# Products with the values by tile shape: one wide and one narrow task per tile instead of two halves of heads

## The chip, the cores and the metric

The kernel runs on one core of one Trainium2 chip. The core has five engines with queues of their own: TensorE (PE, with its weight loads shown as PEld), VectorE (DVE), ScalarE (ACT), GpSimd (POOL) and SyncE (SP), which here only issues transfers. Time is device time of one execution in microseconds (us); the lower the better. Three executions of the kernel before gave 310.41, 311.28 and 312.01 us, so the median is 311.28 us.

## The reference

Block-sparse attention feeds a soft mixture of experts. There are 4 batches, 8 heads, 768 positions in 24 blocks of 32, and a head dimension of 64. A query block sees its own block and both neighbours, the first and the last block, and three sampled blocks; the first and the last query block see everything.

```
scores = scale * q @ k.T                       # scale = 1/8
mask   = |blk_i - blk_j| <= 1, or blk_i or blk_j is 0 or 23, or blk_j in sampled[blk_i]
attn   = softmax(where(mask, scores, -1e9))
x      = (attn @ v)  as [4*768, 8*64]
logits = x @ phi                               # 32 slots: 8 experts x 4
slot_input = softmax(logits, over rows).T @ x
slot_out   = relu(slot_input @ w1[e]) @ w2[e]  # per expert, hidden width 1024
out    = softmax(logits, over slots) @ slot_out
```

Everything is in float32.

## The kernel before

**Tiles and units.** The 22 middle query blocks of a batch go in pairs, called units: 64 queries of all 8 heads. For a unit the kernel gathers the keys of each query block into a staging buffer (`kst`, eight blocks wide: fixed neighbours by POOL, sampled ones by ACT or POOL), multiplies (`s`, line 521), takes maxima, exponentials (`p`) and transposes them on DVE (`ptt`). The three sampled value blocks of a query block are copied into `vrs` by POOL (line 466). The other value blocks are read where they lie, in `v`. Two units make a tile of 128 queries (`T`); the first tile of a batch has one unit and shares its rows with the first and last query blocks, whose dense attention is a task of its own (`avd`). So a batch has five tiles of two units, and four batches have 20.

**Products with the values.** `av_heads(T, rs_)` (line 623) multiplies the turned weights by the values for the heads in `rs_`: `r` is 0 or 1, a half of the heads. The result lies in one PSUM tile `av` of two banks, one for each `g`, which is also the half of PE's rows (partitions 0 to 63 or 64 to 127) that the product uses; each half `r` has its own 130 columns of a bank. The 65th column of each head's values is one, so that the sums of the softmax come out beside the products. Three shapes of matmul follow each other within a call:

- the first and the last value block, for all 128 queries of the tile: shape 64*128 (64 rows, 128 columns of PE's array), lines 628 to 632;
- the two value blocks that both query blocks of a unit see, for 64 queries: shape 64*64, lines 633 to 639;
- the outer neighbour and the three sampled blocks, for 32 queries each: shape 64*32, lines 640 to 656.

A call in the program shows in the profile as two matmuls and two weight loads. The first product into a region has `start`, the last `stop`. Before, `plan_av` (line 658) makes two PE tasks for a tile of two units, one for each half `r`. Each goes through all three shapes. The last tile of the last batch is split in another way (`T.split`) and keeps two halves.

**Order of the work.** The order on each engine is laid out in advance by `Plan.run` (line 94). Every task has a possible engine with an assumed duration, the tasks it depends on, buffers that it takes from pools, and a due number (`key`, with a correction in `BEHIND`). The planner takes the task that can start first by its own reckoning, and among those that could start within 0.03 us the one with the lowest due number. Each engine then runs its tasks in that order and waits for semaphores where the real times differ. The two halves have an assumed PE time of 2.36 us each and the due number n + 0.5; both depend on the turned weights (`T.turned`), on the copies into `vrs` (`T.staged`) and on the batch's values. PE tasks that may come between are the scores of a later unit (due n + 1 and so on), the transposes of finished rows (`mxt`), logits and slot sums. `av` has one buffer, released by the DVE task that divides by the sums (`av_out`, lines 608 to 610). Loads of weights for the mixture are spread over attention and tied to PE tasks of the plan; when attention has ended, its buffers are reused for the remaining weights.

After attention come the experts' two layers and the combination, with weights loaded on the SP queue all the way.

Of the kernel before, what the change touches and what calls it, by code (L numbers as in the profile page):

```python
# [11 lines left out]
F32 = mybir.dt.float32  # L12
I32 = mybir.dt.int32
F32R = mybir.dt.float32r
# [6 lines left out]
BLK, NB, NR = 32, 24, 3  # L21
P = 128
# [6 lines left out]
D1 = D + 1  # L29

VPOS = lambda k: (k - 1) % (NB + 1)
# [48 lines left out]
class Plan:  # L80
# [6 lines left out]
    def add(self, f, opts, deps, key, acq=(), byte=0, pre=None, pace=False):  # L87
        t = Task(f, opts if isinstance(opts, list) else [opts], deps, key, acq, byte, pre, pace)
        kind = self.kinds.setdefault(f.__code__.co_firstlineno, len(self.kinds))
        t.turn = key + BEHIND.get(kind, 0.0)  # L90
        self.tasks.append(t)
        return t
# [96 lines left out]
def attn_moe_kernel(ctx, tc, qT, kT, vfull, vtab, sampled, phi, w1, w2, out):  # L189
    nc = tc.nc  # L190
    PE, ACT, DVE, POOL, SP = nc.tensor, nc.scalar, nc.vector, nc.gpsimd, nc.sync
# [105 lines left out]
    pst = att.enter_context(tc.tile_pool(name="pst", bufs=1))  # L297
# [4 lines left out]
    kst = [pst.tile([P, NP, 256], F32, name=f"kst{n}") for n in range(NKST)]  # L302
    qst = [pst.tile([P, NP, 2, BLK], F32, name=f"q{n}") for n in range(NQ)]

    vrs = [None] * NVR
    for n in range(NVR):
        n = (B * (NB - 2) + n) % NVR
# [57 lines left out]
    add = plan.add  # L365
# [17 lines left out]
    use = []  # L383
# [13 lines left out]
    t_k, t_v, t_first = {}, {}, []  # L397
# [104 lines left out]
    def plan_pair(b, g, n):  # L502
# [73 lines left out]
        if g == 0 or w:  # L576
            plan_av(T, n)
# [7 lines left out]
    def av_out(T, av, lo, hi, rs_=slice(0, 2), xlo=None):  # L585
        n = rs_.stop - rs_.start
        if isinstance(av, list):

            rs = pw.tile([P, 2, 2 * n], F32, tag="rs", name="rs")
            a = [v[lo:hi, 0:4 * D1].rearrange("p (r a d) -> p r a d", r=2, a=2)[:, rs_] for v in av]  # L590
            a = [v.rearrange("p r a d -> p (r a) d") for v in a]
            for g in range(2):
                DVE.tensor_scalar(out=rs[lo:hi, g], in0=a[g][:, :, D], scalar1=EPS, scalar2=None, op0=ALU.add)
            DVE.reciprocal(out=rs[lo:hi], in_=rs[lo:hi])
            x = new_x(T).rearrange("p (g r a d) -> p g r a d", g=2, r=2, a=2)[lo:hi, :, rs_]
            for g in range(2):
                DVE.tensor_tensor(out=x[:, g].rearrange("p r a d -> p (r a) d"), in0=a[g][:, :, 0:D],
                                  in1=rs[lo:hi, g].unsqueeze(2).to_broadcast([hi - lo, 2 * n, D]), op=ALU.mult)
            return
        a = av[lo:hi, :, 0:4 * D1].rearrange("p g (r a d) -> p g r a d", r=2, a=2)[:, :, rs_]  # L600
        x = new_x(T).rearrange("p (g r a d) -> p g r a d", g=2, r=2, a=2)
        x = (x[lo:hi] if xlo is None else x[xlo:xlo + hi - lo])[:, :, rs_]
        if n == 2:
            a, x = (v.rearrange("p g r a d -> p g (r a) d") for v in (a, x))
        else:
            a, x = (v.rearrange("p g r a d -> p (g r) a d") for v in (a, x))
        rs = pw.tile([P, 2, 2 * n], F32, tag="rs", name="rs")
        DVE.tensor_scalar(out=rs[lo:hi], in0=a[:, :, :, D], scalar1=EPS, scalar2=None, op0=ALU.add)  # L608
        DVE.reciprocal(out=rs[lo:hi], in_=rs[lo:hi])
        DVE.tensor_tensor(out=x, in0=a[:, :, :, 0:D],  # L610
                          in1=rs[lo:hi].unsqueeze(3).to_broadcast([hi - lo, 2, 2 * n, D]), op=ALU.mult)

    def av_mm(av, o, m, g, r, lhsT, rhs, start, stop):
        av = av[g][o:o + m] if isinstance(av, list) else av[o:o + m, g]
        PE.matmul(av[:, r * 2 * D1:(r + 1) * 2 * D1].rearrange("p (a d) -> p a d", a=2),  # L615
                  lhsT=lhsT, rhs=rhs, start=start, stop=stop)

    G2 = [(g, slice(64 * g, 64 * g + 64)) for g in range(2)]

    def new_av(T):  # L620
        T.av = psA.tile([P, 2, 512], F32, tag="av", name="av", bufs=1)

    def av_heads(T, rs_):

        vt, us = vtile[T.b], T.units
        one = len(us) == 1
        m = 64 * len(us)
        for n, c in enumerate((4, 5)):
            for r in rs_:
                for g, s_ in G2:  # L630
                    av_mm(T.av, 64 * r if one else 0, m, g, r, T.pt[r][s_, c, 0:m // BLK].rearrange("p j q -> p (j q)"),
                          vt[s_, :, VPOS((0, NB - 1)[n]), r, :], n == 0, False)
        for c in (1, 2):
            for w, u in enumerate(us):
                for r in rs_:
                    for g, s_ in G2:
                        av_mm(T.av, 64 * r if one else 64 * w, 64, g, r,
                              T.pt[r][s_, c, 2 * w:2 * w + 2].rearrange("p j q -> p (j q)"),
                              vt[s_, :, VPOS(2 * u.g + c), r, :], False, False)
        for n in range(NR + 1):  # L640
            for w, u in enumerate(us):
                for r in rs_:
                    for j in range(2):
                        i = 2 * u.g + 1 + j
                        for g, s_ in G2:
                            if n == 0:

                                k, c = (i - 1, 0) if j == 0 else (i + 1, 3)
                                if k in (0, NB - 1):
                                    continue  # L650
                                v_ = vt[s_, :, VPOS(k), r, :]
                            else:
                                c = ((3, 0)[j], 6, 7)[n - 1]
                                v_ = u.vst[j][s_, :, n - 1, r, :]
                            av_mm(T.av, (64 * r if one else 64 * w) + 32 * j, 32, g, r, T.pt[r][s_, c, 2 * w + j], v_,
                                  False, n == NR)

    def plan_av(T, n):
        deps = T.turned + T.staged + [t_v[T.b]]
        use, x_use = [], T.x_use  # L660
        if len(T.units) == 1:
            def both(t):
                new_av(T)
                av_heads(T, range(2))

            def out(t):
                for r in range(2):
                    av_out(T, T.av, 64 * r, 64 * r + 64, slice(r, r + 1), 0)
            t_a = add(both, ("PE", 2.45), deps, n + 0.5, acq=[("av", use)])
            T.out = [add(out, ("DVE", 1.68), [t_a], n + 0.6)]  # L670
        else:

            T.split = T is tiles.get((B - 1, NT - 1))

            def heads(t, r):
                if T.split and r == 0:
                    T.av = [psA.tile([P, 512], F32, tag="s", name="av", bufs=SB) for g in range(2)]
                elif r == 0:
                    new_av(T)
                av_heads(T, (r,))  # L680
            if T.split:
                t_0 = add(lambda t: heads(t, 0), ("PE", 2.36), deps, n + 0.5, acq=[("s", use)] * 2)
                t_a = add(lambda t: heads(t, 1), ("PE", 2.36), [t_0], n + 0.5)
                T.out = [add(lambda t, r=r: av_out(T, T.av, 0, P, slice(r, r + 1)), ("DVE", 1.0), [(t_0, t_a)[r]], n + 0.6,
                             acq=[] if r else [("x", x_use)]) for r in range(2)]
            else:
                t_0 = add(lambda t: heads(t, 0), ("PE", 2.36), deps, n + 0.5, acq=[("av", use)])
                t_a = add(lambda t: heads(t, 1), ("PE", 2.36), [t_0], n + 0.5)
                T.out = [add(lambda t: av_out(T, T.av, 0, P), ("DVE", 1.06), [t_a], n + 0.6, acq=[("x", x_use)])]
        x_use.extend(T.out)  # L690
        use.extend(T.out)
        v_use[T.b].append(t_a)
        T.t_av = t_a
        for u in T.use + list(T.pt_use.values()):
            u.append(t_a)
        if T.t:
            done.append((n, T))
# [343 lines left out]
    m, n = NPRE, first[B - 1]  # L1041
# [70 lines left out]
    t_0 = add(f_row, ("PE", 0.25), [t_m], k, acq=[("pt", u[0])])  # L1112
# [18 lines left out]
    for j, g in enumerate((0, 1, 2, 5)):  # L1131
        t_n = plan_combine(g, N - 4 + j)

        n, p_use, b_use = N + 2 + j, [], []
# [131 lines left out]
    for n in range(2 * NE):  # L1266
# [12 lines left out]
        if n == 6:  # L1279
            g = 3  # L1280
# [154 lines left out]
```

## Time and profile before

| | |
|---|---|
| median of three executions | 311.28 us (310.41 to 312.01) |
| profiled execution, from its first to its last instruction | 312.2 us |
| PE busy with matmuls | 278.2 us (89%) |
| DVE busy | 216.2 us (69%) |
| POOL busy | 185.2 us (59%) |
| ACT busy | 162.1 us (52%) |
| matmuls of line 615 on `v` and `ptt`, busy | 74.8 us, 1728 of them |
| matmuls of line 615 on `vrs` and `ptt`, busy | 47.3 us, 2112 of them |
| mean granted clock of TensorE | 0.979 |

The profile is of one execution; what lies around its span isn't shown apart, and its span stands 0.9 us above the median. A row of a group has the line, engine, operation, tiles (result <- operands), shape and count, then busy time, mean length in ns, and idle time of the engine just before. A row of the timeline has start and length in us, then the same, the count of what is merged in it, and in brackets the idle time before it and what ended it. Matmuls on different positions of the array overlap, so the sum of their lengths is above the busy time. Line numbers are those of the kernel before.

### The profile page before, as it was taken

To read this page: it belongs to the slowest core of one execution; us is meant where nothing else is said; L and a number is where in the kernel's file an instruction comes from. 1 tells how busy PE (TensorE), PEld (TensorE's weight loads), DVE (VectorE), ACT (ScalarE), POOL (GpSimd) and SP (SyncE) were. 2 spreads that over 40 slices of the span, in tenths; PEclk is the share of its full clock that TensorE was granted. 3 is DMA by queue.
4 is the path that set the end of the run, shared out by engine and by line. 5 is a ranking of instruction groups with operands and counts; after the bars stand their busy time and mean duration, and the time that the engine had idled before them with its cause. 6 is when DMAs were issued, how large, how long until landed. Compare 5 with 4: busy or idle time off the path is not lost.

```text
span 312.2 us, 17614 instructions
## 1 busy us (share of the span) xinstructions
PE 278.2 (89%) x7167; PEld 191.7 (61%) x7167; DVE 216.2 (69%) x499; ACT 162.1 (52%) x492; POOL 185.2 (59%) x521
## 2 busy tenths in 40 slices
PE   7689888759999999999999999999999889999750
PEld 6148656536787666777677776877577763466340
DVE  4789967536899879789998778999897253103260
ACT  0766748443367867737667763866761241004250
POOL 2879499772667869958599994847958004000000
PEclk9899999997999999999999999999999999999996
DMA  7935766540045654024475511667779999999998
GB/s 246 399 115 161 208 192 195 152 115 4 19 146 168 196 168 143 7 74 146 138 199 150 141 37 56 154 186 220 207 206 298 354 367 363 413 406 405 391 335 271
DMA packets 33506, 63.62 MB, mean 204 GB/s; under 512 B 5521, under 2 KB 18962, under 8 KB 33426
## 3 DMA queue, kind: packets, MB, share of 16 engines
q1 hardware_dynamic: 33280, 62.37, 62.1%
q8 instruction: 56, 0.92, 1.3%
q14 instruction: 24, 0.20, 0.2%
q10 hardware_dynamic: 146, 0.13, 0.1%
HBM read 56.19 MB, written 6.29 MB: 200 GB/s over the span
## 4 chain that ended last, share of the span: by engine, by line
PE 55%; DVE 14%; DMA 12%; issue 5%; POOL 4%; POOLq 4%; ACT 2%; SPq 1%; ACTq 0%; DVEq 0%
PE av L615 22%; PE s L521 6%; DMA q<-in_qT_dram 5%; PE avd L615 5%; PE pf L1233 5%; PE sd L717 3%; PE pso L1241 3%; DMA w<-in_w_dram 3%; POOLq L347 3%; PE mxt L808 3%; DVE nm L538 3%; DVE ptt L550 2%; DMA v<-in_vfull_dram 2%; DVE x L610 2%; POOL vrs L466 2%
## 5 line engine op out<-in xcount | busy, mean ns | idle before, releaser
L466 POOL COPY vrs<-v 128x260 f32 x264 | 95.5, 407 | 27.1 <-PE av L615 18.3
L543 ACT ACTIVATE p<-s,nm 128x256 f32<-128x256 f32 x176 | 73.4, 479 | 18.8 <-DVE nm L538 15.1
L615 PE MATMUL av<-v,ptt 64*64 64x130 f32 (+2 forms) x1728 | 74.8, 285 | 0.0
L615 PEld LDWEIGHTS av<-v,ptt 64*64 64x64 f32 (+2 forms) x1728 | 50.0, 131 | 27.0 <-issue 19.0
L550 DVE STREAM_TRANSPOSE ptt<-p 128x512 f32<-128x512 f32 x88 | 57.3, 687 | 2.8 <-ACT p L543 2.7
L538 DVE TENSOR_REDUCE nm<-s 128x2 f32<-128x512 f32 x88 | 55.3, 680 | 5.6 <-PE s L521 5.3
L521 PE MATMUL s<-kst,q 64*32 64x256 f32 x1408 | 49.9, 384 | 8.4 <-POOL kst L450 4.9
L442 POOL COPY kst<-ktile 128x384 f32<-128x384 f32 x88 | 42.7, 510 | 13.9 <-PE s L521 12.6
L615 PE MATMUL av<-vrs,ptt 64*32 64x130 f32 x2112 | 47.3, 274 | 3.3 <-issue 3.2
L448 ACT ACTIVATE kst<-ktile 128x128 f32 x162 | 37.4, 304 | 11.0 <-PE s L521 8.4
L521 PEld LDWEIGHTS s<-kst,q 64*32 64x32 f32 x1408 | 28.8, 106 | 20.3 <-POOL kst L450 7.4
L615 PEld LDWEIGHTS av<-vrs,ptt 64*32 64x32 f32 x2112 | 35.6, 105 | 6.1 <-issue 6.0
L450 POOL COPY kst<-ktile 128x128 f32 x102 | 25.6, 296 | 0.6 <-ACT kst L448 0.4
L748 ACT ACTIVATE pd<-sd,nb 128x384 f32<-128x384 f32 x32 | 16.5, 579 | 16.9 <-DVE nb L743 16.4
L615 PE MATMUL avd<-v,ptd 64*64 64x130 f32 x768 | 23.6, 271 | 1.0 <-DVE ptd L752 0.7
L615 PEld LDWEIGHTS avd<-v,ptd 64*64 64x64 f32 x768 | 22.0, 132 | 3.2 <-PE s L521 1.5
L359 ACT COPY xT<-mxt 128x512 f32<-128x512 f32 (+1 forms) x22 | 12.4, 566 | 20.6 <-PE mxt L808 20.6
L485 POOL TENSOR_SCALAR q<-q 128x256 f32<-128x256 f32 x28 | 11.4, 409 | 15.0 <-DMA q<-in_qT_dram 14.8
L717 PE MATMUL sd<-ktile,q 64*32 64x384 f32 x256 | 19.4, 552 | 0.6 <-ACT p L543 0.4
L735 DVE TENSOR_REDUCE nm<-sd 128x1 f32<-128x384 f32 x32 | 16.4, 545 | 3.9 <-PE sd L717 3.9
L483 ACT ACTIVATE q<-q 128x256 f32<-128x256 f32 x20 | 8.3, 417 | 19.5 <-DMA q<-in_qT_dram 19.5
L608 DVE TENSOR_SCALAR rs<-av 128x8 f32<-128x8 f32 (+1 forms) x27 | 4.3, 158 | 19.8 <-PE av L615 19.8
(119 smaller groups left out, 290.2 us busy)
## 6 DMA issues: line engine op xcount, KB each, us to landing
w<-in_w_dram SPq DMA_DIRECT2D x17, 512.0 KB, 10.2
q<-in_qT_dram SPq DMA_DIRECT2D x47, 128.0 KB, 2.8
w<-in_w_dram SPq DMA_DIRECT2D x44, 128.0 KB, 3.6
out_dram<-ob SPq DMA_DIRECT2D x22, 256.0 KB, 4.5
ktile<-in_kT_dram SPq DMA_DIRECT2D x48, 96.0 KB, 2.7
v<-in_w_dram SPq DMA_DIRECT2D x8, 512.0 KB, 11.0
v<-in_w_dram SPq DMA_DIRECT2D x24, 128.0 KB, 3.5
w<-in_w_dram SPq DMA_DIRECT2D x12, 256.0 KB, 6.3
```

The costliest lines, as they stand in the source:

```text
L442: POOL.tensor_copy(out=st[:, :, w:w + 96], in_=kv[:, :, (i - 1) * BLK:(i + 2) * BLK])
L448: ACT.activation(out=st[:, :, o:o + BLK], in_=src, func=AF.Copy, scale=1.0)
L450: POOL.tensor_copy(out=st[:, :, o:o + BLK], in_=src)
L466: POOL.tensor_copy(out=st[:, :, j:j + 1, :], in_=vf[:, :, ds(t.vals[j], 1), :])
L521: PE.matmul(u.s[r][32 * p:32 * p + 32, j, :], lhsT=u.q[s_, p, j, :], rhs=kd[j][0][s_, p, :], start=True, stop=True)
L538: DVE.tensor_reduce(out=u.nm[r], in_=u.s[r], axis=AX.X, op=ALU.max, negate=True)
L543: ACT.activation(out=u.p[r][:, j, :], in_=u.s[r][:, j, :], func=AF.Exp, bias=u.nm[r][:, j:j + 1], scale=1.0)
L550: DVE.transpose(out=T.pt[r][:, :, 2 * w:2 * w + 2, :].rearrange("p k j q -> p j k q"), in_=u.p[r].rearrange("p j (k q) -> p j k q", k=8))
L615: PE.matmul(av[:, r * 2 * D1:(r + 1) * 2 * D1].rearrange("p (a d) -> p a d", a=2), lhsT=lhsT, rhs=rhs, start=start, stop=stop)
L717: PE.matmul(u.s[r][k][32 * p:32 * p + 32, :], lhsT=T.dq.q[s_, p, j, :], rhs=kt[s_, p, 384 * k:384 * (k + 1)], start=True, stop=True)
L735: DVE.tensor_reduce(out=u.nm[r][:, k:k + 1], in_=u.s[r][k], axis=AX.X, op=ALU.max, negate=True)
L748: ACT.activation(out=u.p[r][k], in_=u.s[r][k], func=AF.Exp, bias=u.nb[r], scale=1.0)
```

## The change

A tile of two units that isn't the split one still has two PE tasks. The first goes through the two wide shapes (64*128 and 64*64) for both halves `r`, the second through the narrow shape (64*32) for both. The planner's assumed times are 2.15 and 1.95 us instead of twice 2.36. The first task depends on the turned weights and the values alone; the copies into `vrs` are a dependence of the second.

Since the products of both halves now alternate within one accumulation, the start is made by a product of zeros: one matmul per bank with a 128-column operand of zeros and 260 columns, `start=True`, in the single-pass type float32r; no later product has `start`, and `stop` is on the last of the second half. The tile of zeros is written once by POOL at the beginning. Within the narrow task the order is block, unit, half, query block, bank: the four positions of one unit are used for `r` = 0 and then for `r` = 1 before those of the other unit.

```diff
+    zero = pst.tile([P, P], F32R, name="zero")
+    POOL.memset(zero.bitcast(F32), 0.0)
...
-    def av_heads(T, rs_):
+    def av_heads(T, rs_, wide=True, narrow=True):
...
-        for n, c in enumerate((4, 5)):
+        if wide and len(rs_) == 2 and not one:
+            for g, s_ in G2:
+                PE.matmul(T.av[:, g, 0:4 * D1], lhsT=zero[s_], rhs=zero[s_, 0:1].to_broadcast([64, 4 * D1]), start=True, stop=False)
+        for n, c in enumerate((4, 5) if wide else ()):
...
-                          vt[s_, :, VPOS((0, NB - 1)[n]), r, :], n == 0, False)
-        for c in (1, 2):
+                          vt[s_, :, VPOS((0, NB - 1)[n]), r, :], n == 0 and (one or len(rs_) == 1), False)
+        for c in (1, 2) if wide else ():
...
-        for n in range(NR + 1):
+        for n in range(NR + 1) if narrow else ():
...
-                                  False, n == NR)
+                                  False, n == NR and (one or r == rs_[-1]))
...
-                t_0 = add(lambda t: heads(t, 0), ("PE", 2.36), deps, n + 0.5, acq=[("av", use)])
-                t_a = add(lambda t: heads(t, 1), ("PE", 2.36), [t_0], n + 0.5)
+                def wide(t):
+                    new_av(T)
+                    av_heads(T, range(2), narrow=False)
+                t_0 = add(wide, ("PE", 2.15), T.turned + [t_v[T.b]], n + 0.5, acq=[("av", use)])
+                t_a = add(lambda t: av_heads(T, range(2), wide=False), ("PE", 1.95), [t_0] + T.staged, n + 0.5)
```

## The prediction

> **What bounds the kernel now.** I read the profile's summary first, then the stages, the waits, and last the order of TensorE's work around one tile. TensorE (PE) is the busiest engine, at full granted clock in the middle.
>
> ```profile
> span 312.2 us, 17614 instructions
> PE 278.2 (89%) x7167; PEld 191.7 (61%) x7167; DVE 216.2 (69%) x499; ACT 162.1 (52%) x492; POOL 185.2 (59%) x521
> ...
> 17.00:90.00 73.00, 64.03 (x1892) 45.28 (x1882) 54.26 (x117) 40.35 (x124) 55.53 (x158) 0.98 0.44 125
> 90.00:245.00 155.00, 150.38 (x4606) 110.86 (x4599) 132.28 (x291) 97.97 (x307) 116.67 (x328) 1.00 0.54 156
> ...
> 265.00:290.00 25.00, 24.83 (x326) 13.48 (x322) 4.94 (x13) 4.61 (x11) 0.00 (x0) 1.00 1.03 409
> ```
>
> The lower three rows are busy times of PE, weight loads, VectorE, ScalarE and GpSimd in stretches of the span, then clock, DMA share and GB/s. Attention runs from 17 to 245 us: up to 90 PE is 88% busy (64.03 of 73), from there 97% (150.38 of 155), and VectorE 85%. From 245 the DMA engines are full (share 1.03) with weights whose buffers attention frees. So PE's time between 90 and 245 sets the end of attention, and the tail moves with it one to one.
>
> The list of waits says what PE waits for in the products with the values:
>
> ```profile
> PEld av L615 <- issue: 25.0, 95, 1.1
> PEld s L521 <- POOL kst L450: 7.4, 6, 3.4
> ```
>
> "issue" means that no semaphore was pending. No row has PE waiting for the staged value blocks (vrs). The timeline of weight loads and, below it, of matmuls shows what these 25.0 us are:
>
> ```profile
> 162.84 0.18 PEld L615 LDWEIGHTS av<-v,ptt 64*32 64x32 f32 x16 [0.17 <-issue]
> 162.98 0.76 PEld L615 LDWEIGHTS av<-vrs,ptt 64*32 64x32 f32 x48
> 163.94 1.08 PEld L615 LDWEIGHTS av<-v,ptt 64*128 64x128 f32 x24 [0.20 <-issue]
> 165.20 0.18 PEld L615 LDWEIGHTS av<-v,ptt 64*32 64x32 f32 x16 [0.17 <-issue]
> 165.33 0.47 PEld L615 LDWEIGHTS av<-vrs,ptt 64*32 64x32 f32 x24
> 166.31 0.27 PEld L615 LDWEIGHTS av<-vrs,ptt 64*32 64x32 f32 x20 [0.50 <-issue]
> ```
>
> ```profile
> 114.13 1.71 PE L615 MATMUL av<-v,ptt 64*128 64x130 f32 x40
> 115.63 0.92 PE L615 MATMUL av<-vrs,ptt 64*32 64x130 f32 x48
> 116.30 0.47 PE L521 MATMUL s<-kst,q 64*32 64x256 f32 x8
> ...
> 143.66 5.58 PE L615 MATMUL avd<-v,ptd 64*64 64x130 f32 x192
> ```
>
> Idle of 0.17 to 0.20 us stands wherever the tile shape changes, twice per half. The 0.50 us at 166.31 stands inside one shape: a different thing. If 40 halves pay twice 0.18 (14.4 us), about 10.6 of the 25.0 us are such pauses, 0.5 us for each of 20 two-unit tiles. They sit where a block of code ends:
>
> ```profile
> q8 instruction: 56, 0.92, 1.3%
> ```
>
> ```profile
> 106.56:110.07 3.51, 3.50 (x128) 2.79 (x128) 2.03 (x5) 3.51 (x15) 2.16 (x6) 1.00 0.55 165
> ```
>
> ```profile
> 106.57 0.69 PE L615 MATMUL av<-vrs,ptt 64*32 64x130 f32 x31 [0.17 <-issue]
> 110.57 0.38 PEld L615 LDWEIGHTS av<-vrs,ptt 64*32 64x32 f32 x23 [0.51 <-issue]
> ```
>
> ```profile
> q8 instruction: 1, 0.02, 52.1%
> ```
>
> The first row is of the page's queues, the second of the stretch between two pauses, then the timeline there (matmuls, then loads), last the DMA answer for 107.85 to 108.00 us. PE's code comes in 56 packets of 0.92 MB / 56 = 16 KB; with 2 x 7167 instructions that is 256 each, and between the pauses that end at 106.57 and 110.57 there are exactly 128 matmuls and 128 loads. The 1.30 us before 107.85 have no q8 packet: the next block is fetched from 107.9 and its first instruction runs at 110.57, 2.6 us later. So when PE has nothing in hand, a block of 256 lasts 110.57 - 106.57 = 4.0 us however fast its matmuls are. The block from 162.84 to the pause's end at 166.31 took 3.47 us. I take 3.5 to 4.0 us as the floor of a block.
>
> **The change part by part.** The counts by shape are these:
>
> ```profile
> L615 PE MATMUL av<-vrs,ptt 64*32 64x130 f32 x2112 | 47.3, 274 | 3.3 <-issue 3.2
> L615 PE MATMUL av<-v,ptt 64*64 64x130 f32 x768 | 32.2, 281 | 0.0
> L615 PE MATMUL av<-v,ptt 64*128 64x130 f32 x320 | 28.7, 296 | 0.0
> ```
>
> 320 matmuls of shape 64*128 are 20 two-unit tiles x 2 halves x 8. One of the 20 (the split last one) keeps the old form, so 19 tiles change. Each call is two matmuls and two loads: a half is 24 matmuls in the wide shapes and 64 in the narrow, 176 instructions with the loads.
>
> *Shape changes removed.* A half's wide part lasts 165.20 - 163.94 = 1.26 us, its narrow part 116.30 - 115.38 = 0.92 us before scores of the same shape (115.38 being 114.13 + 1.26 within 0.01), or 163.94 - 162.84 = 1.10 us before another shape: 0.18 us of change. Now a tile costs 2 x (1.26 + 0.92) + 0.18 = 4.54 us. A round of matmuls over four tile positions takes (5.58 - 0.27) / 48 = 0.111 us by the dense row (0.27 is the length of its last matmul). The wide parts are 8 rounds each, so joined they take 1.26 + 8 x 0.111 = 2.15 us.
>
> *Zero products added.* Two single-pass matmuls of 260 columns per tile, on different rows of the array. The nearest rows are these:
>
> ```profile
> 284.83 0.28 PE L1337 MATMUL po<-so,cT 128*128 128x256 f32 x1
> ...
> 286.04 0.97 PE L1337 MATMUL po<-so,cT 128*128 128x256 f32 x6
> ```
>
> ```profile
> masks.py:197 POOL MEMSET ident<- 128x128 f32 x1 | 0.2, 205 | 0.3 <-POOLq L1421 0.3
> ```
>
> ```profile
> 8.54 0.40 POOL L440 COPY kst<-ktile 128x256 f32<-128x256 f32 x1 [2.89 <-DMA ktile<-in_kT_dram]
> ```
>
> (0.97 - 0.28) / 5 = 0.14 us for a 256-column one (0.28 is the length of one alone). If the two overlap, 0.14 us per tile, if not, 0.28; below zero it can't go. I take 0.14, as other matmuls on different rows overlap here. The memset is one of 0.2 us; it lies in GpSimd's 2.89 us wait for the first keys. Without that cover it would cost 0.2 us once.
>
> *The narrow parts joined.* 128 load-matmul pairs. At the pace of a half, 2 x 0.92 = 1.84 us; at the pace of the 48 loads (0.76 / 48 = 15.8 ns a pair) 2.03. I take 1.94, the middle. So a tile costs 2.15 + 0.14 + 1.94 = 4.23 us: 0.31 us less (bounds 2.15 + 0.14 + 1.84 = 4.13 and 2.15 + 0.28 + 2.03 = 4.46: 0.41 to 0.08 less). Times 19: 5.9 us (1.5 to 7.8).
>
> *Code pauses.* The joined narrow part is 128 matmuls and 128 loads: exactly one block, in 1.94 us, against a floor of 3.5. A tile's turn is 352 instructions here, 128 of two scores tasks (1.90 us to the next row at 149.54 below) and some 30 more: two blocks. Boundaries lie anywhere, so I put one 0, 64, 128 and 192 instructions into the narrow part; the other then lies as far behind its end. Time of the 256 before each, at 7.6 ns (narrow), 14.8 ns (scores and others), 2.29 us for the wide 100:
>
> ```profile
> 149.54 1.96 PE L521 MATMUL s<-kst,q 64*32 64x256 f32 x64
> 151.44 1.07 PE L893 MATMUL ms<-x,d 128*32 128x512 f32 x8
> ```
>
> 0: over 4 us, and 1.94: pause 1.56. 64: 4.1, and 1.46 + 0.95 = 2.41: 1.09. 128: 3.7, and 0.97 + 1.90 = 2.87: 0.63. 192: 1.46 + 1.07 (the last 64 of the wide part: 8 rounds and a change) = 2.5, and 0.49 + 1.90 + 0.95 = 3.34: 1.0 + 0.16. Mean 1.1 us a tile; with a floor of 4.0 it is 1.8. Now any 256 hold one half (2.2 to 2.4 us) and 80 others (1.2): 3.4 to 3.6 us, close to the floor, which is why the pauses are short. I take 1.1, the low end, because in the joined wide part the sequencer can run ahead. Against 0.5 now that is +0.6 us a tile (0 if the queue hides it, +1.3 at the other floor).
>
> *What else moves.* The wide task no longer waits for vrs; since PE shows no such wait, it gains nothing. The vrs, the turned weights and the av bank are released at the end of the second task, as now. The narrow task holds the wait for GpSimd; behind it in PE's queue stand the next scores, as behind a half now. No DMA is added. The planner gets 4.10 instead of 4.72 us a tile and will order things differently; no row shows what that is worth. The nearest is a transpose that PE reached too early:
>
> ```profile
> 121.45 0.63 PE L808 MATMUL mxt<-ident,x 128*128 128x128 f32 x4 [0.75 <-DVE x L610]
> ```
>
> One such wait more or less in each of four batches is 3 us either way; I take 0.
>
> *Sum.* +0.6 - 0.31 = +0.29 us a tile. 14 of the 19 tiles lie behind 90 us: 4.1 us. The 5 before it wait 12% of the time anyway, so I count half: 0.7. Together +4.8 us: 312.2 + 4.8 = 317.0 for the profiled execution, which stands 0.9 us above the median of 311.28; on the median, 316.1. I say **316.1 us**.
>
> **The rivals.**
>
> *The code is there in time* (faster). PE's pauses stay at 0.5 us a tile since the sequencer gets far enough ahead. For it: 10.6 us of pauses at some 0.5 are 21, so most of the 56 blocks come without one. Against it: the 0.50 and 0.51 above, which came with only 128 narrow instructions in a row. Then 5.9 us are gained; VectorE at 85% leaves room for that: 305.4 us, or 303.5 at the upper bound. The Trainium skill, Runtime: NRT & Kernel Launch, section Instruction fetch mechanics, is on this side: blocks of 16 KiB, 256 instructions, fetched while the current one runs, the crossing mostly hidden. By that rule the sum would be this rival's; the trace agrees on the block and not on "hidden", with 0.50 us.
>
> *Both cancel* (no change). The pauses grow by 0.3 us a tile, half of my value; or a transpose of another shape lands between the two tasks and gives 0.18 us back on each: 311 us.
>
> *Same position twice* (much slower). In the narrow order of the change, four positions get the first half's products and then the second half's, before the other four positions start. If PE won't look past the second visit, four positions work instead of eight: 3.7 us instead of 1.94, 19 x 1.75 = +33 us: 344 us. Against it: a half's 64 matmuls of 0.27 us in 0.92 us, in pairs on one position, which needs some looking ahead. The skill's TensorE: Matmul & The Clock Gate, Part 3, "What overlaps and what doesn't", has matmuls start strictly in order; no run here shows a second visit.
>
> **How the numbers follow.** Forecast 0.50; in time 0.29; cancel 0.17; same position 0.04. What this kernel's measurement can tell from no change is about 0.5%, 1.6 us. The forecast's own range is 313 to 322: net +0.1 to +0.6 us a tile. The whole range reaches down into the faster case, 305, and up to 322. Slower 0.54, same 0.17, faster 0.29.
>
> **What would show it.** Right: matmul shapes in runs of 18, 32 and 128 a tile, wide parts near 2.3 us, some 40 fewer idles of 0.2 us, and idle marked issue inside narrow runs of 1 us and more, always 256 instructions apart, with PE's time for a tile's turn longer. Wrong: narrow runs of 1.9 us throughout (first rival), or of 3.7 us with no pause (third). Wrong in another way: PE waiting for vrs or kst where it does not now.

## The result

Four executions of the changed kernel gave 319.12 to 324.73 us, median 322.53 us; the kernel before beside it 310.85 us (307.27 to 312.01). The ratio is 1.0367 with a 95% interval of 1.0298 to 1.0437: slower by 3.7%, where 1.5% was forecast (316.1 us), and 0.5 us outside the range. On another chip the same kernel stood at 1.0225 [1.0139, 1.0311]. Medians below are of all executions and ratios leave out disturbed ones, so that the two need not agree exactly.

The page of the profile after (busy times, then tenths of 40 slices):

```profile
span 321.4 us, 17744 instructions
PE 281.4 (88%) x7219; PEld 200.7 (62%) x7219; DVE 219.7 (68%) x502; ACT 161.5 (50%) x491; POOL 184.7 (57%) x520
...
PE   7599879879598999979999998699999889999850
...
PEclk9769999999699999997999999699999999999985
```

TensorE (PE) has holes in slices 10, 17 and 25 (8 us each, counted from 0), and the clock is low in slices 10, 18 and 25. Those are the turnovers from one batch to the next. The same by stretches, first before, then after (length, busy of PE, weight loads, VectorE, ScalarE, GpSimd, then clock, DMA share and GB/s):

```profile
65.00:90.00 25.00, 21.46 (x562) 14.71 (x562) 16.67 (x41) 11.32 (x37) 15.10 (x44) 0.93 0.13 39
...
190.00:215.00 25.00, 24.09 (x796) 18.75 (x785) 22.86 (x52) 14.68 (x43) 16.48 (x46) 1.00 0.56 149
```

```profile
65.00:90.00 25.00, 19.30 (x464) 12.99 (x468) 18.30 (x44) 12.39 (x38) 14.95 (x43) 0.86 0.17 50
...
190.00:215.00 25.00, 21.33 (x590) 15.35 (x596) 18.68 (x45) 10.06 (x27) 13.81 (x40) 0.86 0.34 93
```

At 190 to 215 us PE issues 590 matmuls instead of 796 at a clock of 0.86. From 65 to 90 us it is 464 instead of 562, though there the kernel before has a low clock too (0.93). The loss stands at turnovers, not in every tile. The list of waits after:

```profile
PEld av L617 <- issue: 12.8, 29, 1.4
PEld s L523 <- ACT pd L756: 12.0, 7, 4.4
...
PE s L523 <- ACT pd L756: 9.3, 3, 3.7
```

Issue waits in the products with the values fell from 25.0 us in 95 places to 12.8 in 29, as the change set out to do. New is the wait of the scores (`s`) for ScalarE's exponentials of the dense scores (`pd`): three times, 9.3 us on PE. Before, the same wait was 1.5 us in five places on the weight loads, at most 0.4. The last products of attention, before and after, end at 245.55 and 255.73 us:

```profile
244.59 0.96 PE L615 MATMUL av<-vrs,ptt 64*32 64x130 f32 x46
```

```profile
254.77 0.96 PE L617 MATMUL av<-vrs,ptt 64*32 64x130 f32 x46
```

So attention is 10.2 us longer, and the tail as long as before (312.2 - 245.55 = 66.65, 321.4 - 255.73 = 65.67).

**Tiles.** PE's timeline after, one tile with a long pause and then the narrow task of another without:

```profile
97.15 0.38 PE L632 MATMUL av<-zero 64*128 64x260 f32 x2
97.37 2.17 PE L617 MATMUL av<-v,ptt 64*128 64x130 f32 x48
99.47 1.09 PE L523 MATMUL s<-kst,q 64*32 64x256 f32 x32
...
101.03 1.41 PE L617 MATMUL av<-vrs,ptt 64*32 64x130 f32 x76
103.45 0.53 PE L617 MATMUL av<-vrs,ptt 64*32 64x130 f32 x10 [1.01 <-issue]
...
167.78 0.70 PE L617 MATMUL av<-v,ptt 64*32 64x130 f32 x32
...
169.76 0.37 PE L523 MATMUL s<-kst,q 64*32 64x256 f32 x1
```

Zero products 97.37 - 97.15 = 0.22 us, wide task with them 99.47 - 97.15 = 2.32 us, narrow task 169.76 - 167.78 = 1.98 us: a tile costs 4.30 us against 4.54, 4.6 us less over 19 tiles.

**The turnover.** PE's timeline from the first batch to the second, before and then after:

```profile
70.36 3.60 PE L717 MATMUL sd<-ktile,q 64*32 64x384 f32 x32
...
74.51 1.58 PE L615 MATMUL av<-v,ptt 64*128 64x130 f32 x30
...
77.87 1.58 PE L615 MATMUL av<-v,ptt 64*128 64x130 f32 x30
...
80.14 1.52 PE L717 MATMUL sd<-ktile,q 64*32 64x384 f32 x31
...
84.76 2.13 PE L521 MATMUL s<-kst,q 64*32 64x256 f32 x64
86.83 0.44 PE L615 MATMUL avd<-v,ptd 64*64 64x130 f32 x4
```

```profile
74.43 2.23 PE L725 MATMUL sd<-ktile,q 64*32 64x384 f32 x31
76.59 1.37 PE L617 MATMUL av<-v,ptt 64*64 64x130 f32 x36
...
78.74 0.66 PE L816 MATMUL mxt<-ident,x 128*128 128x128 f32 x4
79.33 1.52 PE L725 MATMUL sd<-ktile,q 64*32 64x384 f32 x32
84.52 4.13 PE L523 MATMUL s<-kst,q 64*32 64x256 f32 x64 [3.67 <-ACT pd L756]
88.58 6.17 PE L617 MATMUL avd<-v,ptd 64*64 64x130 f32 x192
...
144.14 2.43 PE L523 MATMUL s<-kst,q 64*32 64x256 f32 x32 [1.92 <-ACT pd L756]
146.50 0.48 PE L892 MATMUL md<-ident,dT 128*128 128x128 f32 x1
...
203.29 4.13 PE L523 MATMUL s<-kst,q 64*32 64x256 f32 x64 [3.67 <-ACT pd L756]
```

Each batch begins with two dense scores tasks (`sd`), each of which takes four score buffers until ScalarE has made its exponentials. Before, the last tile's two halves (from 74.51 and 77.87) lay between the two tasks (70.36 and 80.14). Now both (74.43 and 79.33) come behind that tile, with only a one-unit tile and its transposes (76.59 to 79.33) between them. When the second is done all score buffers are held, and the next scores find none. All engines at that place:

```profile
79.33 1.52 PE L725 MATMUL sd<-ktile,q 64*32 64x384 f32 x32
82.55 1.02 DVE L743 TENSOR_REDUCE nm<-sd 128x1 f32<-128x384 f32 x2
83.88 2.15 ACT L756 ACTIVATE pd<-sd,nb 128x384 f32<-128x384 f32 x4 [3.70 <-DVE nb L751]
```

VectorE begins the maxima of the second task 1.70 us after the matmuls' end and ScalarE the exponentials at 83.88; PE goes on at 84.52. After the wait the granted clock is low for some microseconds: 64 score matmuls take 88.58 - 84.52 = 4.06 us, against 86.83 - 84.76 = 2.07 before. The stretch of these matmuls, and then one of the kernel before:

```profile
84.52:88.58 4.06, 4.06 (x65) 1.91 (x65) 3.49 (x8) 2.95 (x9) 1.93 (x6) 0.50 0.11 30
```

```profile
70.36:73.96 3.60, 3.60 (x34) 2.17 (x34) 2.15 (x5) 0.49 (x4) 1.89 (x6) 0.53 0.02 5
```

The clock is 0.50 in the first. The second is the first dense scores task of the second batch, 3.60 us at a clock of 0.53: the kernel before has a low clock at this turnover too, on other matmuls. The three turnovers cost 9.3 us of waiting, 2.0 us of slow scores at two of them and 2.36 - 1.04 = 1.3 at the middle one (half as many scores, against half of 2.07): 14.6 us.

**Code pauses.** Counted over attention: gaps in PE's records (matmuls, loads and semaphores, numbered from the start) that stand at record 193 of 256 with no semaphore pending, less 0.2 us where the shape changes and 0.015 where not, 17 to 250 us. Before 8.3 us, after 7.2 us. The changed kernel's profile on the other chip has about 8, so that 1 us more or less means little. The sum is then -4.6 (tiles) - 1.1 (pauses) + 14.6 (turnovers) = +8.9 us of the 10.2 us. The other 1.3 us stand already at the end of the first batch's dense products, 30.0 us against 28.68, and were not followed further.

The sum comes out better than its parts do. From one end of the dense products to the next, and from the last to the end of attention, the kernel before takes 64.45, 56.11, 54.81 and 41.50 us, and the change 64.75, 60.20, 58.91 and 41.87. The first turnover is priced at 5.7 us, like the third, but its stretch is only 0.3 us longer; and the last stretch, with shorter tiles and no turnover, is not shorter. So that the whole comes within 1.3 us is in part chance; the comparison with E5 below is the sounder one.

### The profile page after: what moved, and what is told of

Its sections match the earlier page's. It is cut to its first block, busy times and chain, and to the rows that moved or that the text cites. A ratio compares the mean times of both kernels' runs of the same rounds, so it can differ in the third digit from the quotient of the medians.

```text
span 321.4 us, 17744 instructions
## 1 busy us (share of the span) xinstructions
PE 281.4 (88%) x7219; PEld 200.7 (62%) x7219; DVE 219.7 (68%) x502; ACT 161.5 (50%) x491; POOL 184.7 (57%) x520
## 4 chain that ended last, share of the span: by engine, by line
PE 58%; DVE 10%; DMA 8%; issue 6%; POOLq 4%; POOL 4%; ACT 4%; SPq 2%; ACTq 1%; DVEq 0%
PE av L617 18%; PE s L523 10%; PE avd L617 7%; DMA q<-in_qT_dram 5%; PE pf L1241 4%; PE pso L1249 4%; POOLq L349 4%; PE sd L725 3%; PE mxt L816 2%; DVE x L612 2%; DVE ptd L760 2%; DMA ktile<-in_kT_dram 2%; PE po L1345 2%; PE st L383 2%; POOL vrs L468 2%
## 5 line engine op out<-in xcount | busy, mean ns | idle before, releaser
L523 PE MATMUL s<-kst,q 64*32 64x256 f32 x1408 | 56.6, 418 | 14.7 <-ACT pd L756 9.3
L617 PE MATMUL av<-v,ptt 64*64 64x130 f32 (+2 forms) x1728 | 65.1, 280 | 0.0
L552 DVE STREAM_TRANSPOSE ptt<-p 128x512 f32<-128x512 f32 x88 | 57.9, 690 | 10.3 <-ACT p L545 10.1
L617 PEld LDWEIGHTS av<-v,ptt 64*64 64x64 f32 (+2 forms) x1728 | 52.5, 133 | 13.2 <-issue 6.8
L540 DVE TENSOR_REDUCE nm<-s 128x2 f32<-128x512 f32 x88 | 56.1, 680 | 6.9 <-PE s L523 6.4
L617 PE MATMUL av<-vrs,ptt 64*32 64x130 f32 x2112 | 45.3, 276 | 4.3 <-issue 4.3
L617 PEld LDWEIGHTS av<-vrs,ptt 64*32 64x32 f32 x2112 | 38.5, 105 | 6.3 <-issue 6.0
L617 PEld LDWEIGHTS avd<-v,ptd 64*64 64x64 f32 x768 | 23.1, 139 | 3.4 <-DVE nm L540 1.6
L485 ACT ACTIVATE q<-q 128x256 f32<-128x256 f32 x25 | 10.4, 420 | 21.7 <-DMA q<-in_qT_dram 21.6
L487 POOL TENSOR_SCALAR q<-q 128x256 f32<-128x256 f32 x23 | 9.3, 406 | 19.0 <-DMA q<-in_qT_dram 19.0
L361 ACT COPY xT<-mxt 128x512 f32<-128x512 f32 (+1 forms) x19 | 10.6, 557 | 13.2 <-PE mxt L816 13.2
L612 DVE TENSOR_TENSOR x<-av,rs 128x512 f32<-128x512 f32 (+1 forms) x27 | 16.5, 611 | 0.9
## 6 DMA issues: line engine op xcount, KB each, us to landing
w<-in_w_dram SPq DMA_DIRECT2D x17, 512.0 KB, 10.2
v<-in_w_dram SPq DMA_DIRECT2D x8, 512.0 KB, 10.2
```

What stands on the lines that cost most here:

```text
L523: PE.matmul(u.s[r][32 * p:32 * p + 32, j, :], lhsT=u.q[s_, p, j, :], rhs=kd[j][0][s_, p, :], start=True, stop=True)
L540: DVE.tensor_reduce(out=u.nm[r], in_=u.s[r], axis=AX.X, op=ALU.max, negate=True)
L552: DVE.transpose(out=T.pt[r][:, :, 2 * w:2 * w + 2, :].rearrange("p k j q -> p j k q"), in_=u.p[r].rearrange("p j (k q) -> p j k q", k=8))
L612: DVE.tensor_tensor(out=x, in0=a[:, :, :, 0:D], in1=rs[lo:hi].unsqueeze(3).to_broadcast([hi - lo, 2, 2 * n, D]), op=ALU.mult)
```

## The experiments

Two theories stood first: the planner's new order at the turnovers makes the loss, or the joined form itself does, through code pauses.

**E1 to E4: the planner's two entries, apart from the matmuls.** E1 is the change with the old assumed times and the old dependence on the copies into `vrs`:

```diff
-t_0 = add(wide, ("PE", 2.15), T.turned + [t_v[T.b]], n + 0.5, acq=[("av", use)])
-t_a = add(lambda t: av_heads(T, range(2), wide=False), ("PE", 1.95), [t_0] + T.staged, n + 0.5)
+t_0 = add(wide, ("PE", 2.36), deps, n + 0.5, acq=[("av", use)])
+t_a = add(lambda t: av_heads(T, range(2), wide=False), ("PE", 2.36), [t_0], n + 0.5)
```

> The wide and the narrow task with the planner's old entries (2.36 us each, and the first task depends on the copies into vrs as well), so that every engine gets the task order of the kernel before. Theory O (order: the loss comes from the planner's new order around the dense scores, where PE waits 2.2 to 4.2 us three times): no such wait, and the time falls below the kernel before by what the removed shape changes are worth, 0.2 to 0.4 us on 19 tiles, so 303 to 307 us against 311. Theory C (code: the joined narrow run makes PE wait for its instructions): the loss stays, 316 to 322 us.

312.45 us against 316.01 on that chip, ratio 0.9893 [0.9836, 0.995]. With the old order the loss is gone, as theory O has it; the gain, 3.3 us by the ratio, is a little under the 0.2 to 0.4 us on 19 tiles that I expected. Attention ends at 245.5 us, as before, with 13.5 us of code pauses: -4.6 + 5.2 = +0.6 us by the terms above, 0.0 measured. The profile's shorter span (309.5 us against 312.2) lies behind attention, where the change alters nothing, so it isn't shown that the new matmuls make the 1.1%.

E2 restores the dependence alone, E3 the assumed times alone:

```diff
-t_0 = add(wide, ("PE", 2.15), T.turned + [t_v[T.b]], ...)    # E2
+t_0 = add(wide, ("PE", 2.15), deps, ...)
-("PE", 2.15) ... ("PE", 1.95)                                # E3
+("PE", 2.36) ... ("PE", 2.36)
```

> The changed kernel with one of its two planner entries undone: assumed times 2.15 and 1.95 us as in the change, but the wide task depends on the copies into vrs again. Theory O: if the assumed times make the bad order, 317 to 323 us and the long PE waits for the dense exponentials stay; if the missing dependence makes it, 303 to 309 us. Theory C: no difference to the change, 317 to 322 us, with the same pauses inside narrow runs.

> The other entry undone: assumed times 2.36 us each, the wide task free of the copies into vrs as in the change. Theory O: if the missing dependence makes the bad order, 317 to 323 us; if the assumed times do, 303 to 309 us. Theory C: no difference to the change, 317 to 322 us.

E2: 307.91, 309.64, 315.00 and 321.49 us, too scattered for a ratio; in its profile PE doesn't wait for the exponentials of the dense scores, attention ends at 240.9 us, pauses 9.7 us. E3: 315.79 us, 0.989 [0.9777, 1.0002], unclear. Its profile has the second dense scores behind the one-unit tile, just ahead of the next scores, at the middle turnover only, and the stretch between the dense products' ends there is 61.4 us, against 56.1 (149.24 - 93.13) before. But PE waits only 0.15 us for the exponentials there, and the profiled execution took 319.11 us, the longest of ten (the shortest took 308.40), so this shows the order and not what it costs. I had expected one entry to bring the whole loss. The assumed times alone (E2) don't, and the dependence alone (E3) moves the dense scores at one turnover of three.

E4 is the kernel before with the new assumed times:

```diff
-t_0 = add(lambda t: heads(t, 0), ("PE", 2.36), deps, ...)    # t_a alike
+t_0 = add(lambda t: heads(t, 0), ("PE", 2.15), deps, ...)    # t_a: 1.95
```

> The kernel before, two halves as they were, with nothing but the assumed times changed to 2.15 and 1.95 us. Theory O, if the assumed times make the order: slower than before by 4 to 10 us, 315 to 321 us, with PE waits of over 2 us after the dense scores, though no matmul has changed. Theory C: as before, 309 to 313 us.

315.11 us against 316.01, no ratio (310.27 to 321.91); span 311.4 us, the dense scores in their old place. The expectation missed: wrong assumed times alone cost nothing that shows.

The planner reads assumed times, dependences and buffers, not matmuls. So E1 has the order of the kernel before, and E2 and E4 share one order (ScalarE runs the same 486 instructions in one sequence). E2 and E4 differ in the matmuls alone: attention ends at 240.9 us in E2 and 246.1 in E4. That is 5.2 us less, where the tiles give -4.6 and the pauses +0.3 (9.7 against 9.4).

**E5 and E6: the order itself.** E5 is the change with one dependence more: the last tile's wide task comes behind the first dense scores of the next batch.

```diff
     t_0 = add(wide, ("PE", 2.15), T.turned + [t_v[T.b]], n + 0.5, acq=[("av", use)])
+    T.t_first = t_0
...
     qks[n] = t_qk
+    if j == 0 and b:
+        tiles[b - 1, NT - 1].t_first.deps.append(t_qk)
```

> The changed kernel with both of its planner entries and one dependence added: from the second batch on, the last tile's wide task comes behind the first dense scores task of the next batch, as it stood in the kernel before. Nothing else is given back. Theory O (the loss is the place of the dense scores): the three waits of 2.2 to 4.2 us go, attention ends 8 to 13 us earlier than with the change, 307 to 312 us where the change has 320 to 323. Rival P (the loss lies in the new tasks themselves or in many small moves of the order): less than 3 us is regained.

E6 forces the late dense scores on the old halves; no matmul changes.

```diff
+behind = [tiles[b - 1, NT - 1].t_av] if j == 0 and b else []
-t_qk = add(..., [T.dq.t, t_k[b], t_q0], n, acq=s_acq)
+t_qk = add(..., [T.dq.t, t_k[b], t_q0] + behind, n, acq=s_acq)
```

> The kernel before, with its two halves, and one dependence added: from the second batch on, the first dense scores task comes behind the last tile of the batch before, as the change's order has it. No matmul and no assumed time is changed. Theory O: PE waits 2 to 4 us behind the second dense scores task of each of three batches, and the time is 8 to 13 us above the kernel before. Rival P: within 2 us of the kernel before.

E5: 311.52 us against 314.7, ratio 0.9928 [0.9885, 0.9971], beside a ratio of 1.0225 for the unchanged change on the same chip: this one dependence regains 3.0% of some 314 us, about 9 us. E6: 332.46 us, ratio 1.0585 [1.0496, 1.0674]. The order alone, without one new matmul, costs 18 us, more than the 8 to 13 that I expected. PE's timeline of E5 and then of E6:

```profile
70.69 1.52 PE L726 MATMUL sd<-ktile,q 64*32 64x384 f32 x32
72.14 0.38 PE L632 MATMUL av<-zero 64*128 64x260 f32 x2
72.36 2.79 PE L617 MATMUL av<-v,ptt 64*128 64x130 f32 x72
...
76.57 1.80 PE L726 MATMUL sd<-ktile,q 64*32 64x384 f32 x28
...
81.03 0.65 PE L523 MATMUL s<-kst,q 64*32 64x256 f32 x13
...
242.34 0.96 PE L617 MATMUL av<-vrs,ptt 64*32 64x130 f32 x46
```

```profile
79.41 2.20 PE L717 MATMUL sd<-ktile,q 64*32 64x384 f32 x31
...
84.28 1.52 PE L717 MATMUL sd<-ktile,q 64*32 64x384 f32 x32
89.46 3.60 PE L521 MATMUL s<-kst,q 64*32 64x256 f32 x64 [3.66 <-ACT pd L749]
```

In E5 a whole tile (72.14 to 76.57) lies between the two dense tasks and the scores start at once. In E6 the old halves show the same 3.66 us wait and slow scores as the change. E5's attention ends at 242.34 + 0.96 = 243.30 us: -4.6 for the tiles and 10.0 - 8.3 = +1.7 for pauses make -2.9, measured 243.30 - 245.55 = -2.25.

Against the change, which has the same matmuls, E5's four stretches are 4.3, 2.2, 4.5 and 0.4 us shorter, so each turnover gives back most of its price (5.7, 3.2 and 5.7). In all 14.6 us less E5's 2.8 us more of pauses make 11.8, measured 255.73 - 243.30 = 12.4. In E6 the three waits (9.2 us) and the slow scores behind them come to 13.5 us; the rest, 4.0 us of it in the last stretch, which has no turnover, was not followed.

Each added dependence also moved other tasks: ScalarE runs 495 instructions in E5 and 491 in the change, 482 in E6 and 492 before. So E5 and E6 show what the order costs; that most of it stands at the dense scores is read from the traces.

**E7: is the low clock a cost of its own?** The change, with 14, 7 and 14 matmuls of the identity into a spare bank behind the second dense scores, so that PE doesn't stand idle:

```diff
             if j and b:
+                fb = bank("fb")
+                for m in range((0, 14, 7, 14)[b]):
+                    PE.matmul(fb[:, 0, :], lhsT=ident, rhs=ident, start=True, stop=True)
```

> The changed kernel with matmuls of the identity put behind the second dense scores task of batches 2, 3 and 4 (14, 7 and 14 of them, about 3.6, 1.8 and 3.6 us), so that PE works while it would wait there; they compute nothing that is used. If part of the loss is the lower clock that the trace shows for the scores behind the wait (two scores tasks in 4.06 us instead of 1.89), the scores there fall back to 1.9 us and 2 to 6 us of the loss are regained. If the clock costs nothing beyond the wait, the time stays within 1.5 us of the change, or grows where the fillers are longer than the wait.

```profile
81.17 3.39 PE L730 MATMUL fb<-ident 128*128 128x128 f32 x28
84.90 2.67 PE L523 MATMUL s<-kst,q 64*32 64x256 f32 x64 [0.34 <-ACT pd L760]
87.50 5.59 PE L617 MATMUL avd<-v,ptd 64*64 64x130 f32 x192
```

```profile
84.90:87.50 2.60, 2.60 (x65) 1.25 (x65) 2.57 (x7) 2.08 (x6) 1.34 (x4) 1.00 0.00 0
```

The scores behind the wait take 87.50 - 84.90 = 2.60 us at a clock of 1.00, instead of 4.06 at 0.50, though they begin as late as without the fillers. So about 1.5 us of each long wait's price is the clock. The time doesn't show it: 321.29 us or 1.0216 [1.0126, 1.0306] can't be told from the unchanged change's 1.0225 [1.0139, 1.0311], and the 2 to 6 us expected were not regained. Attention ends at 255.7 us in both profiles. The three stretches with a turnover are together 2.5 us shorter, and the last is 3.5 us longer, with 10.1 us of code pauses in all against 7.2. The one look at the change on this chip, beside E5 to E7:

> The changed kernel as it is, on the same chip as the three others, for comparison: 3 to 4% above the kernel before on this chip.

It gave 323.49 us (319.58 to 326.97) and the ratio of 1.0225 used above, a little under the 3 to 4% expected.

**E9 and E10: does the place of the block boundaries decide?** E5 with 16, 32 and 48 matmuls of one column more at the start (64, 128 and 192 instructions), and the kernel before with 32:

```diff
+        if t is not None:
+            for j in range(32):
+                PE.matmul(st[:, 0, 0:1], lhsT=ident, rhs=ident[:, 0:1], start=True, stop=True)
```

> The changed kernel with the dense scores in their old place, and 64 one-column matmuls and loads more on PE at the very beginning, while it waits for the first data: every later block boundary falls 64 instructions earlier in the work. Theory K (code pauses are real and depend on where a boundary falls): the pauses inside narrow runs move to other places, their sum differs from the 10 us of the unshifted kernel by up to 5 us, attention's end moves with it at most one to one. Rival N (the pauses are something else): same places, same sum, within 1 us of the unshifted kernel.

> As before with 128 instructions instead of 64. Theory K: another set of pauses; over the four placements the sum averages what the joined narrow runs cost, by the prediction 0.5 to 1.1 us a tile, 10 to 21 us, against 8 to 10 with halves. Rival N: no difference.

> As before with 192 instructions. Theory K and rival N as for 64 and 128.

> The kernel before, halves and all, with 128 instructions more at the beginning. Theory K: the pauses (8.3 us in its profile) move and their sum changes by a few us, less than in the joined form, since any 256 instructions hold some wide work; the time within 3 us of the kernel before. Rival N: no difference.

As times these missed: ratios 1.001 [0.9957, 1.0064], 1.0292 [1.0166, 1.0419], 1.0548 [1.0415, 1.068] and 1.0272 [1.0157, 1.0388], but the added matmuls held up the first batch. Its dense products end at 31.3, 38.3 and 45.5 us instead of E5's 29.0, and E10's at 38.57 instead of 28.68. What can be read is the sum of pauses: 10.4, 11.0 and 10.5 us against 10.0 in E5. So in this order the joined form pays about 10 us wherever its boundaries fall, as rival N has it for the sum; with other orders it paid 7.2 us (the change) and 13.5 (E1). In the halves the sum went from 8.3 us to 1.3 us, against rival N and by more than I expected for theory K, so there the place seems to decide, by this one run.

## Why the prediction was right or wrong

"Slower" was right for a reason that was wrong, which is luck. The 4.8 us were to come from code pauses in every tile; the loss came from the turnovers between batches.

- **Shape changes removed, narrow parts joined** (4.54 to 4.23 us a tile): right. Measured 4.30; wide task 2.32 against 2.15 + 0.14, narrow 1.98 against 1.94, read from one tile each; E2 against E4 points the same way. The gain was 4.6 us instead of 5.9, inside its bounds of 1.5 to 7.8.
- **Zero products** (0.14, at most 0.28): 0.22 us.
- **Same position twice**, the rival at 344 us: fell. The narrow task of 128 matmuls took 1.98 us and not 3.7, on all eight positions.
- **Code pauses** (+0.6 us a tile, 11 us over 19): the mechanism was right, the size was not. The longest single pauses grew from 1.1 to 1.5 us, always at 256-instruction boundaries. But the sum was 7.2 us in the change, 10.0 in E5 and 13.5 in E1 against 8.3: -1.1 to +5.2 us. The floor of 3.5 to 4.0 us for a block, read where the DMA engines were half busy, isn't one: blocks of 2.4 to 2.6 us went through without a pause (below).
- **The planner "will order things differently; no row shows what that is worth ... I take 0"**: this is the step that failed. The bound of 3 us came from one transpose's wait of 0.75 us in each batch, the wrong neighbour. The dense scores hold all score buffers, so their place costs a wait for a chain through VectorE and ScalarE (up to 3.67 us on PE) and then the clock: 14.6 us by the trace, where the prediction has 0 and at most 3. With the dense scores back in place (E5) attention ended 12.4 us earlier and about 9 us of the time came back. The steps "the wide task no longer waits for vrs ... it gains nothing" and "4.10 instead of 4.72 us" were costed on PE alone; both are inputs of the planner, and together they made the order.
- **The tail moves one to one**: right, 65.67 against 66.65 us.
- **PE waiting for vrs or kst** as the other way to go wrong: PE waited for the exponentials of the dense scores, which I hadn't named.

With the order put right, the answer would have been a little faster: E1 at 0.9893 and E5 at 0.9928 gain 1.1% and 0.7%, 3.3 and 2.2 us of 311, between the rivals "code is there in time" (5.9 us) and "both cancel". Both intervals lie below 1, though E1's gain doesn't stand in attention itself. Either is to be kept rather than the two kernels.

Open is why the planner moves the dense scores at all three turnovers when both entries change, at one with the dependence alone and at none with the assumed times alone (E1 to E4). It takes what can start first by its own reckoning, and I have not followed that reckoning.

## What to carry to other kernels

A change that also edits a list scheduler's assumed times or dependences is two changes: run the new instructions under the old order first, and cost the new order by listing what each stage's turnover does with the scarce buffers. When two tasks together take all buffers of a pool, the work that lies between them is what hides their release; moving that work away cost a chain through other engines at each turnover here, however small the change to the tasks themselves. Add to such a wait what the matmuls behind it lose: here 64 of them took 4.06 us instead of 2.07, of which 1.5 us was the clock, though taking that away (E7) did not shorten the whole.

## What the runs showed of the hardware

**Short blocks of code paused where the DMA engines were busy.** I had expected the pause to follow from the block's length alone. Blocks of 256 PE instructions with under 3 us of work of their own, in attention of the change, E1, E2 and E5: 12 with a DMA share under 0.25 had pauses of 0.15 us on average (one of them 0.84); 32 with a share above that had 0.77 us. Five of the change, from one block's first instruction to the next's (length, busy times, clock, DMA share, GB/s):

```profile
190.98:193.40 2.42, 2.42 (x129) 2.42 (x128) 0.92 (x3) 0.00 (x0) 2.02 (x7) 1.00 0.00 0
182.37:184.96 2.59, 2.59 (x132) 2.39 (x133) 1.72 (x4) 1.96 (x9) 2.13 (x6) 1.00 0.00 0
125.50:127.80 2.30, 2.30 (x132) 2.06 (x130) 2.09 (x4) 2.25 (x9) 2.30 (x8) 1.00 0.38 118
99.92:103.45 3.53, 2.52 (x140) 2.09 (x124) 3.28 (x6) 3.17 (x10) 2.00 (x6) 1.00 0.45 122
44.74:48.47 3.73, 2.54 (x137) 2.19 (x130) 1.64 (x3) 2.96 (x9) 3.53 (x11) 1.00 0.55 149
```

The first two have no transfers and no pause; the last two have pauses of 1.28 and 1.46 us. The third shows that the instructions don't decide: the same block, with the same instructions ahead of it, had 0.25 us here and 1.35 us in E5, where the DMA share was 0.60. This is read from traces side by side; no run changed the transfers alone, and some blocks with busy DMA engines had no pause, so the cause is argued and not shown. It would explain why the sum of pauses moved so much between kernels whose tiles are the same.

**The clock after a wait.** Behind a wait of 3.67 us the next 64 score matmuls took 4.06 us at a granted clock of 0.50, twice in the changed kernel, against 2.07 us at 1.00 before. With matmuls on a spare bank during the wait they took 2.60 us at 1.00, so 0.5 us of the difference is not the clock's.
